# Converting the weights two units at a time, each pair joined in its own raw bytes

## The chip, the core and the metric

One core of a Trainium2 chip. The metric is the device time of one execution in microseconds. The kernel before takes 903.28 us (median of three runs, 903.13 to 905.31). All times below come from one profiled execution of it or from these runs. Five engines work beside each other and are synchronised by semaphores: TensorE (PE) multiplies matrices, VectorE (DVE) and ScalarE (ACT) work on elements, GpSimd (POOL) does the sums and maxima over partitions, and SyncE (SP) issues the transfers (DMAs). Each takes its own instructions strictly in the order in which they were written down.

## What is computed

An attention with a decay, whose result is the input of a layer that takes the maximum of three products:

```python
scores = scale * np.matmul(q, k.transpose(0, 1, 3, 2))       # 8 batches, 8 heads, 576 x 64
cum = np.cumsum(np.log(np.clip(f, 0.0001, 1.0)), axis=-1)
scores = np.where(causal, -1000000000.0, scores + cum[:, :, :, None] - cum[:, :, None, :])
attn = np.exp(scores - np.max(scores, axis=-1, keepdims=True))
attn = attn / (np.sum(attn, axis=-1, keepdims=True) + 1e-09)
x = np.matmul(attn, v)                                       # seen as [4608, 512]
h = np.maximum(np.maximum(x @ w1, x @ w2), x @ w3)           # w1, w2, w3: [512, 768]
out = (h @ w_out).astype(np.float32)                         # w_out: [768, 512]
```

The four weights arrive as float64, everything else as float32.

## The kernel before

**Weights.** They are read as pairs of int32 and cut into 24 units of 128 x 512 values: 18 of w1, w2 and w3 (four row blocks of 128 x 128 columns each; unit `step` belongs to matrix `step % 3` and column block `step // 3`) and 6 of w_out (128 rows each). `load_weights` handles one unit a call: a DMA of 0.5 MB brings the raw words into the unit's own slot `w0` to `w23` (L511); ACT rescales the top words (a Prelu, L515); DVE shifts the low words into a small tile `x` (L517) and joins top and low there to a float32 value (L519); ACT copies the value, rounded to the matmul's format, as the unit's high part (L522); DVE subtracts that from the value for the low part (L523). `x` is one of two tiles that take turns, named `o` and `hdl` in the profile. Both parts are written over the slot's raw words, which are dead by then. Each product of the last layer is three matmuls: high x high, high x low, low x high (L964 for w1 to w3, L993 for w_out).

**Attention of the first batch.** The weights are needed from the first batch's layer on, and are converted while its eight heads (numbers 0 to 7) run. A head comes in two units: unit 2, queries 0 to 255, and unit 1, the other 320, itself in two halves, first "b" (banks `s11` and `s12`), then "a" (bank `s10`). Each part is a chain over the engines: PE's first pass makes the scores (L647), DVE takes the maximum over the blocks (`mx`, L704 and L707), POOL the maximum over the partitions (`gm`, an all-reduce, L717), PE's second pass subtracts it (`s<-gm`, L647), ACT takes the exponential (`pf`, L735), PE multiplies by the values (`t` or `mp`, L772), and ACT copies the result and its sum out (`u` L784, `ph` L786). The q and k of the eight heads are read raw into the last eight weight slots and turned by PE and copied (L481 on DVE, L483 on ACT) into the tiles `ks`, `qs`, `xh` and `xl`; the last two heads' copies go to `xl`.

**The order.** A planner in Python lists steps with engine, cost in ns, keys that they read and write, and a priority; `emit` simulates the engines with these costs and writes the steps down by their simulated start. So a changed cost or key shifts steps of every engine's program. In the simulation an engine takes the ready step of the lowest priority number; weights have `WP + WR * step`, heads `n * 0.5 - LEAD`. Twenty warm-up matmuls (L453) with priority 90 fill places where PE would be idle in that simulation. SP issues all DMAs in order; an issue that must wait for a slot holds those behind it.

```python
LEAD, MLAG, WP, WR = 2.1, -0.1, 0.7, 0.65
for n in range(H):
    retire([f"raw{n}/0", f"raw{n}/1"], [f"w{NW - H + n}"])
for wstep in range(4 * FT):
    load_weights(wstep, WP + WR * wstep)
```

## Time and profile before

| | before |
|---|---|
| time, median of three runs | 903.28 us (903.13 to 905.31) |
| span of the profiled execution | 900.3 us |
| around the span (903.28 − 900.3) | 3.0 us |
| HBM read / written | 50.22 MB / 9.87 MB |
| weight units, each one DMA | 24 of 0.5 MB |
| conversion of the weights | first Prelu at 24.87 us, last subtraction at 109.2 us |

The profiled execution's own time was not recorded beside its span; the span is set against the median. "Busy" is the time in which an engine has an instruction under way; the instructions of one engine overlap by their ends, so the pitch from one start to the next is shorter than a duration. A row of a timeline shows start, duration, engine, line, operation, what is written and read, shapes, a count where equal neighbours were joined and, in brackets, idle time ahead of it with the engine that ended it.

### The profile page before, as it was taken

The numbers are of one execution on the slowest core, as the hardware profiler recorded it, in microseconds if no ns is written. First come the engines' busy times: TensorE is split into PE (matmuls) and PEld (weight loads), VectorE is DVE, ScalarE is ACT, GpSimd is POOL, SyncE is SP. The second block draws the span as 40 slices with busy tenths as digits, with TensorE's granted clock in tenths as the row PEclk, the third lists the DMA queues.
The fourth block names the chain that finished last, engine by engine and source line by source line (L and its number), as shares of the span: only waits on it lengthen the run. The fifth ranks groups of instructions, "written<-read, shape, count | busy, mean of one in ns | idle before, by whom it ended". The sixth has DMA issues, their size and how long they took to land.

```text
span 900.3 us, 18339 instructions
## 1 busy us (share of the span) xinstructions
PE 889.3 (99%) x6646; PEld 804.0 (89%) x6646; DVE 624.8 (69%) x1419; ACT 389.0 (43%) x904; POOL 425.8 (47%) x380
## 2 busy tenths in 40 slices
PE   8999999999999999999999999999999999999998
PEld 6899989888889899989989998998989898998998
DVE  6999954667759786877849787786958677672211
ACT  6898543433334443443334443344433533442111
POOL 4543232245555756556464755555565564650000
PEclk9999999999999999999999999999999999999999
DMA  7994265554464454446445445536434555401000
GB/s 197 316 270 133 56 159 131 147 135 127 99 189 96 124 136 118 126 100 169 96 124 149 117 133 138 140 93 181 95 102 123 126 149 118 105 15 37 1 36 24
DMA packets 98155, 110.99 MB, mean 123 GB/s; under 512 B 52637, under 2 KB 65693, under 8 KB 98066
## 3 DMA queue, kind: packets, MB, share of 16 engines
q1 hardware_dynamic: 98066, 109.83, 46.7%
q8 instruction: 53, 0.87, 0.4%
q14 instruction: 36, 0.29, 0.1%
HBM read 50.22 MB, written 9.87 MB: 67 GB/s over the span
## 4 chain that ended last, share of the span: by engine, by line
PE 92%; ACT 3%; DMA 1%; DVE 1%; SPq 1%; issue 1%; DVEq 0%; ACTq 0%
PE mp L964 51%; PE mp L993 17%; PE s L647 12%; PE t L803 9%; PE t L772 2%; PE t L822 1%; DMA w<-in_moe_w_dram 1%; ACT w L515 1%; ACT pf L735 1%; SPq L368 1%; DMA r_r<-rdram 0%; ACT ph L786 0%; ACT w_r L522 0%; PE s L663 0%; ACT u L784 0%
## 5 line engine op out<-in xcount | busy, mean ns | idle before, releaser
L964 PE MATMUL mp<-xh_r,w_r 128*128 128x320 f32 (+1 forms) x2160 | 463.5, 298 | 1.7 <-DVE tm L973 1.4
L964 PEld LDWEIGHTS mp<-xh_r,w_r 128*128 128x128 f32 x2160 | 356.1, 188 | 11.2 <-issue 5.6
L964 PE MATMUL mp<-xl_r,w_r 128*128 128x320 f32 (+1 forms) x1080 | 319.6, 296 | 0.4 <-DVE xl_r L940 0.4
L759 POOL PARTITION_ALL_REDUCE z<-va_s x96 | 194.9, 2030 | 158.4 <-DVE va_s L751 57.4
L717 POOL PARTITION_ALL_REDUCE gm<-mx x131 | 156.6, 1196 | 206.8 <-DVE mx L707 88.9
L964 PEld LDWEIGHTS mp<-xl_r,w_r 128*128 128x128 f32 x1080 | 203.3, 188 | 1.1 <-DVE xl_r L940 0.6
L973 DVE TENSOR_TENSOR tm<-mp,tm 128x256 f32<-128x256 f32 (+1 forms) x192 | 86.5, 451 | 84.6 <-PE mp L964 79.4
L647 PE MATMUL s<-qs_r,ks_r 128*128 128x320 f32 (+4 forms) x784 | 133.1, 284 | 0.2 <-issue 0.2
L647 PEld LDWEIGHTS s<-qs_r,ks_r 128*128 128x128 f32 (+1 forms) x784 | 116.9, 181 | 18.2 <-issue 13.4
L993 PE MATMUL mp<-w_r,hmh_r 128*128 128x512 f32 (+1 forms) x396 | 122.7, 392 | 0.0
L707 DVE TENSOR_TENSOR mx<-mx,s 128x320 f32<-128x320 f32 (+3 forms) x248 | 92.3, 372 | 19.5 <-PE s L647 6.9
L993 PEld LDWEIGHTS mp<-w_r,hmh_r 128*128 128x128 f32 x396 | 70.2, 188 | 13.2 <-issue 1.4
L976 ACT ACTIVATE hmh_r<-tm 128x256 fp32r<-128x256 f32 x96 | 39.9, 416 | 97.0 <-DVE tm L973 96.1
L993 PE MATMUL mp<-w_r,hml_r 128*128 128x512 f32 (+1 forms) x198 | 76.8, 388 | 0.0
L971 ACT ACTIVATE tm<-mp 128x256 f32<-128x256 f32 (+1 forms) x96 | 39.6, 413 | 82.3 <-PE mp L964 78.0
L536 DVE STREAM_TRANSPOSE hl<-hl 128x576 f32<-128x576 f32 x56 | 68.7, 1242 | 8.1 <-DMA hl<-in_k_dram 5.3
L735 ACT ACTIVATE pf<-s 128x512 f32<-128x512 f32 (+4 forms) x107 | 49.4, 506 | 30.5 <-PE s L647 26.4
L978 DVE TENSOR_TENSOR hml_r<-tm,hmh_r 128x256 fp32r<-128x256 f32 x96 | 48.2, 502 | 18.5 <-ACT hmh_r L976 17.9
L720 POOL CAST qs_r<-gm 1x256 fp32r<-1x256 f32 (+1 forms) x112 | 56.0, 500 | 7.2
L676 DVE TENSOR_TENSOR s<-s,mask 128x256 f32<-128x256 f32 x96 | 40.8, 425 | 25.8 <-PE s L647 25.5
L714 ACT ACTIVATE mx<-s 128x320 f32<-128x320 f32 (+1 forms) x64 | 26.7, 417 | 58.4 <-DVE s L681 45.1
L735 ACT ACTIVATE ph_f<-s 128x384 f32<-128x384 f32 x80 | 36.1, 505 | 36.1 <-PE s L647 36.1
(209 smaller groups left out, 1227.9 us busy)
## 6 DMA issues: line engine op xcount, KB each, us to landing
qs_r<-hl SPq DMA_DIRECT2D x168, 144.0 KB
ks_r<-hl SPq DMA_DIRECT2D x168, 144.0 KB
w<-in_moe_w_dram SPq DMA_DIRECT2D x18, 512.0 KB
out_dram<-o_r SPq DMA_DIRECT2D x35, 256.0 KB
hl<-in_q_dram SPq DMA_DIRECT2D x14, 576.0 KB
hl<-in_k_dram SPq DMA_DIRECT2D x14, 576.0 KB
r_r<-rdram SPq DMA_DIRECT2D x56, 144.0 KB
vn<-in_v_dram SPq DMA_DIRECT2D x30, 128.0 KB
```

The costliest lines, as they stand in the source:

```text
L536: add("DVE", 1085, lambda e=e, tt=tt, xs=xs: nc.vector.transpose(tt[:, e], xs[:, e]), [key + "0"], [key + "1"], prio)
L647: nc.tensor.matmul(bank[bk][0:l.shape[-1], col:col + w], l, rhs(qa, w), start=start and bk not in begun, stop=stop, skip_group_check=True)
L707: nc.vector.tensor_tensor(mt[:, a:a + w], mt[:, a:a + w], bank[bk][:, col:col + w], op=ALU.max)
L717: add("POOL", 450 + 2.6 * nq, lambda: nc.gpsimd.partition_all_reduce(gm, mt, P, bass.bass_isa.ReduceOp.max), [km, km + "a"], [kg], prio - CB)
L720: add("POOL", 130 + 0.9 * nq, lambda: nc.gpsimd.tensor_copy(QS(s)[96:97, 1, q0:q0 + nq], gm[96:97, :]), [kg], [kx], prio - CB)
L735: add("ACT", act_cost(w), lambda bk=bk, w=w, col=col: nc.scalar.activation(px()[:, col:col + w], bank[bk][:, 0:w], AF.Exp, scale=sc), [kb[ ...
L759: add("POOL", 520 + 5.1 * nq, lambda: nc.gpsimd.partition_all_reduce(Z[:, q0:q0 + nq], blocks_sum()[:, q0:q0 + nq], P, bass.bass_isa.Reduc ...
L803: nc.tensor.matmul(t[D * j:D * j + D, qa:qa + w], vn[:, j, c, 0:D], prs[j][0]()[:, col:col + w], start=x == 0, stop=True, skip_group_check ...
L964: nc.tensor.matmul(m, unit_w(i, fb)[:, w, kt, :], xx, start=kt == 0 and x == 0, stop=kt == KT - 1 and x == 2,)
L973: add("DVE", dve_cost(cn), lambda m=m: nc.vector.tensor_tensor(t, m, t, op=ALU.max), [km, kt_], [kt_], prio)
L978: add("DVE", dve_cost(w), lambda hh=hh, hl=hl, a=a, d=d, w=w: nc.vector.tensor_tensor(hl()[:, fb, d:d + w], t[:, a:a + w], hh()[:, fb, d:d ...
L993: nc.tensor.matmul(mp[:, 0:cn], l[:, fb, cs], unit_o(fb)[:, r, ds], start=fb == 0 and x == 0, stop=fb == FT - 1 and x == 2,)
```

## The change

The 24 slots become 12 of twice the size. A step now converts two units at once, the two neighbouring column blocks of one matrix (or two row blocks of w_out): eleven such steps, and a function `load_last` that handles the last two units of w_out singly. For a double step:

- one DMA of 1 MB (13 weight DMAs in all instead of 24) brings the raw words into slot `step + 1`;
- the Prelu, the shift, the join, the copy and the subtraction take 1024 columns each;
- the shift writes onto the low words that it reads (every second word), and the join writes the values into the first half of the same slot, so no tile `x` is used;
- the two parts are written into slot `step`, the one beside it, whose raw words were the previous step's.

So a step's split must wait for the previous step's split, and slot 11 gets raw words twice: those of step 10, and then those of the last two units, whose DMAs wait for step 10's conversion; these two use the tiles `x` as before. The order in which the steps are listed to the planner is kept, with priority `WP + 2 * WR * step`, and the costs are those of 1024 columns; for the shift in place the cost is 0.53 ns a column.

```diff
     NW = 3 * FT + FT
-    RAW = [sb(f"w{i}", [P, 1024], I32) for i in range(NW)]
+    NW2 = NW // 2
+    RAW2 = [sb(f"w{i}", [P, 2, 1024], I32) for i in range(NW2)]
+    RAW = [RAW2[i // 2][:, i % 2] for i in range(NW)]
...
+    def convert(x, low, top, kt, kl, kx, prio):
+        n = x.shape[-1]
+        add("ACT", act_cost(n) + 40, lambda: nc.scalar.activation(
+            top.bitcast(F32), top.bitcast(F32), AF.Prelu, scale=2.0 ** -112, alpha=2.0 ** 32), [kt], [kt], prio)
+        y = low if kl == kt else x
+        add("DVE", 0.53 * n + 60 if y is low else 0.85 * n, lambda: nc.vector.tensor_scalar(
+            y, low, 29, None, op0=ALU.logical_shift_right), [kt], [kl], prio)
+        add("DVE", 1.1 * n + 60, lambda: nc.vector.scalar_tensor_tensor(
+            x, top, 3, y, op0=ALU.logical_shift_left, op1=ALU.bitwise_or), [kt, kl], [kx], prio)
+
+    def split(x, h, l, kx, kh, kl, gone, prio):
+        n = x.shape[-1]
+        add("ACT", act_cost(n) + 40, lambda: nc.scalar.activation(h(), x.bitcast(F32), AF.Copy), kx, [kh] + gone, prio)
+        add("DVE", 1.1 * n + 60, lambda: nc.vector.tensor_tensor(
+            l(), x.bitcast(F32), h().bitcast(F32), op=ALU.subtract), kx + [kh], [kl], prio)
...
-        PD = 12
-        raw, x = RAW[step], XW[step % len(XW)]
+        PD = 6
+        raw, key = RAW2[step + 1].rearrange("p t x -> p (t x)"), f"w{step + 1}"
+        x = raw[:, 0:1024]
         after = [f"wh{step - PD}"] if step >= PD else []
...
-            add("SP", 560, lambda: nc.sync.dma_start(out=cols(raw), in_=src.bitcast(I32)[:, :, 2 * c0:2 * c1]),
-                after, [key], DPW + 0.01 * step, 524288 / 360)
+            add("SP", 560, lambda: nc.sync.dma_start(
+                out=raw.rearrange("p (c x) -> p c x", c=n), in_=src.bitcast(I32)),
+                after, [key], DPW + 0.02 * step, 1048576 / 360)
             pair = raw.rearrange("p (x t) -> p x t", t=2)
-            top, low = pair[:, :, 1], pair[:, :, 0]
-            add("ACT", act_cost(512) + 40, lambda: nc.scalar.activation(
-                top.bitcast(F32), top.bitcast(F32), AF.Prelu, scale=2.0 ** -112, alpha=2.0 ** 32), [key], [key], prio)
-            add("DVE", 335, lambda: nc.vector.tensor_scalar(
-                x, low, 29, None, op0=ALU.logical_shift_right), [key], [kx], prio)
-            add("DVE", 602, lambda: nc.vector.scalar_tensor_tensor(
-                x, top, 3, x, op0=ALU.logical_shift_left, op1=ALU.bitwise_or), [key, kx], [kx], prio)
-        val = cols(x.bitcast(F32))
-        add("ACT", act_cost(512) + 40, lambda: nc.scalar.activation(half(0), val, AF.Copy), [kx], [kh, key], prio)
-        add("DVE", 602, lambda: nc.vector.tensor_tensor(half(1), val, half(0).bitcast(F32), op=ALU.subtract),
-            [kx, kh], [kl], prio)
+            convert(x, pair[:, :, 0], pair[:, :, 1], key, key, key, prio)
+        split(x, lambda: both(step)[:, 0], lambda: both(step)[:, 1], [key], f"wh{step}", f"wl{step}", [f"w{step}"], prio)
+
+    def load_last(prio):
+        step = NW2 - 1
+        for e in range(2):
+            raw, x = RAW[2 * step + e], XW[e]
...
+                add("SP", 560, lambda raw=raw, src=src: nc.sync.dma_start(out=raw, in_=src.bitcast(I32)),
+                    [], [key, f"w{step}"], DPW + 0.02 * step, 524288 / 360)
+                pair = raw.rearrange("p (x t) -> p x t", t=2)
+                convert(x, pair[:, :, 0], pair[:, :, 1], key, kx, kx, prio + 0.5 * e)
+        for e in range(2):
+            split(XW[e], lambda e=e: unit_o(FT - 2 + e)[:, 0], lambda e=e: unit_o(FT - 2 + e)[:, 1],
+                  [f"x{e}"], f"wh{step}/{e}", f"wl{step}/{e}", ["wu0", "wu1"], prio + 0.5 * e)
...
-    for wstep in range(4 * FT):
-        load_weights(wstep, WP + WR * wstep)
+    for wstep in range(NW2 - 1):
+        load_weights(wstep, WP + 2 * WR * wstep)
+    load_last(WP + 2 * WR * (NW2 - 1))
```

PE's program holds the same matmuls as before. The order differs from about 25 us to about 250 us of the old trace, on every engine. Three places of it follow; a row has the line in the code, the operation, the tile that is written, `<-`, the tiles that are read (names with a running number) and the shape.

On ACT, at the first unit of the weights (in the old trace at 24.87 us), before:

```order
L483 ACTIVATE xl_70<-mp1_131 64x288
L515 ACTIVATE w0_95<-w0_95 128x512
L483 ACTIVATE xl_70<-t_129 64x288 x2
L483 ACTIVATE xl_70<-mp2_132 64x288
L515 ACTIVATE w1_96<-w1_96 128x512
L522 ACTIVATE w0_r_447<-o_120 128x512
L784 ACTIVATE u0_88<-t_129 64x160
```

and after, where L495, L501 and L812 are the old L483, L515 and L784:

```order
L495 ACTIVATE xl_70<-mp1_119 64x288
L495 ACTIVATE xl_70<-t_117 64x288 x2
L495 ACTIVATE xl_70<-mp2_120 64x288
L501 ACTIVATE w1_96<-w1_96 128x1024
L812 ACTIVATE u0_88<-t_117 64x160
L814 ACTIVATE ph1_79<-t_117 1x160
```

The copies of the last turned heads now stand ahead of the first Prelu, and there is one Prelu where there were two.

On DVE, around the maxima of head 4 "b" (`s11`, `s12`) and head 3 "a" (`s10`), in the old trace from 52.00 to 58.31 us, before:

```order
L519 SCALAR_TENSOR_TENSOR o_120<-w6_101,o_120 128x512
L704 TENSOR_REDUCE mx1_82<-s11_126 128x160
L707 TENSOR_TENSOR mx1_82<-mx1_82,s12_127 128x160
L707 TENSOR_TENSOR mx1_82<-mx1_82,s12_127 128x64
L523 TENSOR_TENSOR w5_r_711<-hdl_119,w5_r_711 128x512
L523 TENSOR_TENSOR w6_r_727<-o_120,w6_r_727 128x512
L517 TENSOR_SCALAR hdl_119<-w7_102 128x512
L517 TENSOR_SCALAR o_120<-w8_103 128x512
L519 SCALAR_TENSOR_TENSOR hdl_119<-w7_102,hdl_119 128x512
L519 SCALAR_TENSOR_TENSOR o_120<-w8_103,o_120 128x512
L704 TENSOR_REDUCE mx1_82<-s10_125 128x160
L707 TENSOR_TENSOR mx1_82<-mx1_82,s10_125 128x32
```

and after, where L504, L506 and L512 are shift, join and subtraction, L732 and L735 the maximum, and a slot number counts pairs:

```order
L504 TENSOR_SCALAR w7_102<-w7_102 128x1024
L506 SCALAR_TENSOR_TENSOR w6_101<-w6_101 128x1024
L506 SCALAR_TENSOR_TENSOR w7_102<-w7_102 128x1024
L504 TENSOR_SCALAR w8_103<-w8_103 128x1024
L890 TENSOR_SCALAR hdl_107<-mp2_120 128x8
L732 TENSOR_REDUCE mx1_82<-s11_114 128x160
L735 TENSOR_TENSOR mx1_82<-mx1_82,s12_115 128x160
L735 TENSOR_TENSOR mx1_82<-mx1_82,s12_115 128x64
L891 RECIPROCAL hdl_107<-hdl_107 128x8
L512 TENSOR_TENSOR w4_r_714<-w5_100,w4_r_714 128x1024
L732 TENSOR_REDUCE mx1_82<-s10_113 128x160
L735 TENSOR_TENSOR mx1_82<-mx1_82,s10_113 128x32
```

Ahead of the maximum on `s10` stand 9 shifts, 9 joins and 7 subtractions of one unit before, and 8, 7 and 5 of two units now; between the two maxima stand six instructions of one unit before, and now a reciprocal and one subtraction of two.

On PE, between the second pass of head 4 "b" and that of head 3 "a" (in the old trace 58.36 to 61.64 us), before:

```order
L647 MATMUL s12_127<-gm1_84,pl2_72 128x64
L964 MATMUL mp0_130<-pl1_xa_665,w0_r_447 128x256
L964 MATMUL mp0_130<-u4_92,w0_r_447 128x256
L964 MATMUL mp0_130<-pl1_xa_665,w0_r_447 128x256
L772 MATMUL mp2_132<-hmh_86,va1_78 65x128
L772 MATMUL mp2_132<-hmh_86,va1_78 65x256
L964 MATMUL mp0_130<-pl1_xa_665,w0_r_447 128x256
L964 MATMUL mp0_130<-u4_92,w0_r_447 128x256
L964 MATMUL mp0_130<-pl1_xa_665,w0_r_447 128x256
L647 MATMUL s11_126<-xh_69 128x160 x3
L647 MATMUL s10_125<-gm1_84,pl2_72 128x160 x3
L647 MATMUL s10_125<-gm1_84,pl2_72 128x32
```

and after, where L675, L800 and L886 are the old L647, L772 and L858:

```order
L800 MATMUL t_117<-pf1_80,hdh_76 65x160 x4
L886 MATMUL mp2_120<-hdl_107,rx_109 128x128 x2
L675 MATMUL s11_114<-gm1_84,pl2_72 128x160 x3
L675 MATMUL s12_115<-gm1_84,pl2_72 128x160
L675 MATMUL s12_115<-gm1_84,pl2_72 128x64
L675 MATMUL s10_113<-gm1_84,pl2_72 128x160 x3
L675 MATMUL s10_113<-gm1_84,pl2_72 128x32
L886 MATMUL mp2_120<-hdl_107,rx_109 128x128 x2
L675 MATMUL s11_114<-xh_69 128x160 x3
```

The two second passes, with other work between them before, now follow each other directly.

More of the change, by code (lines that the diff above doesn't have):

```diff
@@ L348, in blocks_sum, with both, key_w, key_o @@
         return lazy("va1", [P, S], F32, "s")
+    def both(s):
+        return lazy(f"w{s}", [P, 2, 1024])
     def unit_w(i, fb):
-        return lazy(f"w{3 * fb + i}", [P, 2, KT, P])
+        return both(3 * (fb // 2) + i).rearrange("p t (c e x) -> p t c e x", c=KT, e=2)[:, :, :, fb % 2]
     def unit_o(fb):
-        return lazy(f"w{3 * FT + fb}", [P, 2, DM])
+        return both(3 * FT // 2 + fb // 2).rearrange("p t (e x) -> p t e x", e=2)[:, :, fb % 2]
+    def key_w(i, fb):
+        return [f"{c}{3 * (fb // 2) + i}" for c in ("wh", "wl")]
+    def key_o(fb):
+        s = 3 * FT // 2 + fb // 2
+        return [f"{c}{s}" + f"/{fb % 2}" * (s == NW2 - 1) for c in ("wh", "wl")]
     TM = [sb(f"tm{i}", [P, S1]) for i in range(2)]
@@ L1062 @@
     for n in range(H):
-        retire([f"raw{n}/0", f"raw{n}/1"], [f"w{NW - H + n}"])
-    for wstep in range(4 * FT):
-        load_weights(wstep, WP + WR * wstep)
+        retire([f"raw{n}/0", f"raw{n}/1"], [f"w{(NW - H + n) // 2}"])
+    for wstep in range(NW2 - 1):
+        load_weights(wstep, WP + 2 * WR * wstep)
+    load_last(WP + 2 * WR * (NW2 - 1))
     fbs = range(FT)
```

28 lines of the change are left out of this document (13 added, 15 removed).

## The prediction

> **What bounds the kernel now.** I read the head of the page first, then the table of busy times by stretch, then what TensorE waits for.
>
> ```profile
> span 900.3 us, 18339 instructions
> PE 889.3 (99%) x6646; PEld 804.0 (89%) x6646; DVE 624.8 (69%) x1419; ACT 389.0 (43%) x904; POOL 425.8 (47%) x380
> PE 92%; ACT 3%; DMA 1%; DVE 1%; SPq 1%; issue 1%; DVEq 0%; ACTq 0%
> ```
>
> TensorE (PE) is busy for 99% of the span and makes 92% of the chain that ends last. A change that leaves PE's 6646 matmuls alone, as this one does, can only move the 11 us in which PE is idle, or add to them. The first two lines say how much room there is, not where.
>
> ```profile
> core 0: us, PE busy (x) PEld busy (x) DVE busy (x) ACT busy (x) POOL busy (x), PEclk, DMA share, GB/s
> 0.00:25.00 25.00, 21.81 (x262) 17.17 (x263) 16.26 (x37) 14.56 (x32) 12.03 (x31) 1.00 0.75 215
> 25.00:64.00 39.00, 36.99 (x296) 34.32 (x295) 36.72 (x75) 37.08 (x83) 21.14 (x22) 1.00 1.05 287
> 64.00:110.00 46.00, 46.00 (x398) 45.93 (x398) 42.22 (x95) 32.24 (x75) 14.46 (x15) 1.00 0.38 113
> 110.00:900.30 790.30, 784.54 (x5697) 706.57 (x5695) 529.62 (x1216) 305.07 (x716) 378.20 (x313) 1.00 0.44 113
> ```
>
> The averages of 69% for VectorE (DVE) and 43% for ScalarE (ACT) hide the stretch that matters. From 25 to 64 us, where the weights are converted between the first batch's heads, DVE is busy for 36.72 of 39.00 us and ACT for 37.08, and PE loses 39.00 − 36.99 = 2.0 us. From 64 to 110 it loses nothing, and the 5.8 us behind 110 lie where the conversion is over. PE's granted clock is 1.00 everywhere.
>
> ```profile
> PE t L772 <- ACT pf L735: 1.1, 2, 0.5
> PE t L772 <- ACT xl L483: 0.6, 1, 0.6
> PE s L647 <- ACT pf L735: 0.3, 1, 0.3
> ```
>
> These are PE's waits from 20 to 70 us, and they are the 2.0 us: exponentials that ACT delivers late, and once the copies of the last two turned heads. What the change can gain stands in these rows.
>
> **What the conversion costs by itself.** The pitch of neighbours (start to start) is the price of an instruction in a full queue, since the durations overlap.
>
> ```profile
> 47.18 1.25 ACT L515 ACTIVATE w<-w 128x512 f32<-128x512 f32 x2
> 70.97 0.64 ACT L522 ACTIVATE w_r<-hdl 128x512 fp32r<-128x512 f32 x1
> 71.48 0.64 ACT L522 ACTIVATE w_r<-o 128x512 fp32r<-128x512 f32 x1
> L522 ACT ACTIVATE w_r<-o x12: 612/632/645, 28.4 to 103.4; 128x512 fp32r<-128x512 f32 x12
> L540 ACT ACTIVATE hl<-hl x28: 1152/1171/1195, 31.9 to 751.9; 128x1152 fp32r<-128x1152 f32 x28
> ```
>
> ACT at 512 columns: two Prelus take 1.25 us and one 0.68, so the pitch is 0.57; the copy's is 71.48 − 70.97 = 0.51. From 512 to 1152 columns the median rises from 632 to 1171 ns, 0.84 ns a column, so 512 more cost 0.43. A Prelu of 1024 is then 1.00 (two of 512: 1.14) and a copy 0.94 (1.02). A pair saves 0.22 us, eleven pairs **2.4 us of ACT**.
>
> ```profile
> 54.29 0.68 DVE L523 TENSOR_TENSOR w_r<-hdl,w_r 128x512 fp32r<-128x512 f32 x1
> 54.89 0.94 DVE L523 TENSOR_TENSOR w_r<-o,w_r 128x512 fp32r<-128x512 f32 x1
> 55.76 0.42 DVE L517 TENSOR_SCALAR hdl<-w 128x512 int32<-128x512 int32 x1
> 56.09 0.42 DVE L517 TENSOR_SCALAR o<-w 128x512 int32<-128x512 int32 x1
> 56.43 0.68 DVE L519 SCALAR_TENSOR_TENSOR hdl<-w,hdl 128x512 int32<-128x512 int32 x1
> 57.03 0.68 DVE L519 SCALAR_TENSOR_TENSOR o<-w,o 128x512 int32<-128x512 int32 x1
> L519 DVE SCALAR_TENSOR_TENSOR o<-w,o x12: 678/689/1093, 26.0 to 101.7; 128x512 int32<-128x512 int32 x12
> L542 DVE SCALAR_TENSOR_TENSOR hl<-hl x28: 1284/1350/1762, 33.1 to 754.9; 128x1152 fp32r<-128x1152 f32 x28
> ```
>
> DVE at 512: shift 0.34 (55.76, 56.09, 56.43), join 0.60 (56.43, 57.03, 57.63), subtraction 0.60 (54.29, 54.89). From 689 to 1350 ns over 640 columns is 1.03 a column, 0.53 for 512 more: join and subtraction of 1024 cost 1.13 each (two of 512: 1.20). The shift runs at twice that pace; if it keeps it, 512 more columns cost 0.27 and it takes 0.61 (two: 0.68). A pair saves 0.21, eleven **2.3 us of DVE**. But the new shift writes onto the words it reads, 8 bytes apart, and no row shows such an instruction. At the pace of one column a time it takes as long as a join, 1.13, which is 0.52 worse. I take 0.61, since the nearest row, the same operation reading the same words 8 bytes apart, has it at the double pace; 1.13 is the other end.
>
> [...]
>
> **The front: one wait goes.**
>
> ```profile
> 24.87 0.68 ACT L515 ACTIVATE w<-w 128x512 f32<-128x512 f32 x1 [4.03 <-DMA w<-in_moe_w_dram]
> 28.39 0.61 ACT L522 ACTIVATE w_r<-o 128x512 fp32r<-128x512 f32 x1
> 58.94 0.36 PE L964 MATMUL mp<-pl_xa,w_r 128*128 128x256 f32 x1
> ```
>
> ACT waits 4.03 us for the first unit, with the `xl` copies queued behind it for which PE waits 0.6. The new order has these copies ahead of the first Prelu, so this stall goes. The first DMA is now 1 MB; at the 287 GB/s of the stretch its second half lands 0.52 / 0.287 = 1.8 us later, near 26.7. That costs nothing: the first split stands at 28.39 and PE's first matmul on a weight at 58.94, 30 us later.
>
> ```profile
> L523 DVE TENSOR_TENSOR w_r<-hdl,w_r x12: 676/684/1144, 37.7 to 109.2; 128x512 fp32r<-128x512 f32 x12
> L993 PE MATMUL mp<-w_r,hmh_r x396: 278/394/505, 118.4 to 896.4; 128*128 128x512 f32 x186, 128*128 128x256 f32 x12
> ```
>
> At the other end the last two units' DMAs must now wait on SP until slot 11 is free of step 10's raw words, and the small loads of the heads' sums queue behind them. The last unit was done at 109.2 and the first matmul on w_out starts at 118.4, so 9 us cover it; beyond these, a late unit costs PE what it is late. I cost it at nothing.
>
> **The middle: DVE is late for the heads' maxima.** The order shows the weights' work moved ahead of the maxima of the last heads. The place is the second pass of head 3 "a" (`s10<-gm`).
>
> ```profile
> 57.63 0.65 DVE L704 TENSOR_REDUCE mx<-s 128x160 f32<-128x480 f32 x1
> 58.31 0.19 DVE L707 TENSOR_TENSOR mx<-mx,s 128x32 f32<-128x32 f32 x1
> 58.36 0.75 PE L647 MATMUL s<-gm,pl 128*128 128x160 f32 x5
> 58.67 1.29 POOL L717 PARTITION_ALL_REDUCE gm<-mx  x1 [0.46 <-DVE mx L707]
> 61.64 0.62 PE L647 MATMUL s<-gm,pl 128*128 128x160 f32 x4
> 62.62 0.69 DVE L523 TENSOR_TENSOR w_r<-hdl,w_r 128x512 fp32r<-128x512 f32 x1 [0.66 <-ACT w_r L522]
> 63.84 0.88 PE L772 MATMUL t<-pf,hdh 128*65 128x32 f32 x6 [0.53 <-ACT pf L735]
> 63.69 0.19 DVE L863 RECIPROCAL hdl<-hdl 128x8 f32<-128x8 f32 x1
> 63.80 0.60 DVE L704 TENSOR_REDUCE mx<-s 128x160 f32<-128x480 f32 x1
> ```
>
> Ahead of the maximum at 57.63 the old order has 9 shifts, 9 joins and 7 subtractions: 9 × 0.34 + 16 × 0.60 = 12.7 us. The new one has 8, 7 and 5 of double size: 8 × 0.61 + 12 × 1.13 = 18.4. So DVE reaches it 5.8 us later by its own work, while PE has about as much ahead of the pass as before (some 330 matmuls into its program in both). Against this stand the slack of 61.64 − (58.67 + 1.29) = 1.7, and DVE's idle time that the work can fill: 2.28 in the stretch, less the 0.66 at 62.62 that lies behind, 1.6. The pass is late by 5.8 − 1.7 − 1.6 = 2.5 us; PE's stall of 0.53 at 63.84 is then absorbed, which leaves **+2.0 us**. If none of the idle time can be filled it is +3.6.
>
> A second count, without the slack: in the old order PE has six matmuls on w0, a head's values and a first pass between head 4 b's second pass and this one, 2.7 us (58.94 to 61.64); in the new order it has nothing. DVE has there a reciprocal, a subtraction of 1024 and the maximum: 0.11 (63.69 to 63.80) + 1.13 + 0.65 + 0.11 = 2.0, against 58.94 − 58.36 = 0.58 of PE. Were head 4 b just in time, PE would still wait 1.4; less 0.53 that is +0.9, my lower end. Behind 64 us PE's idle time is nil already, so what is lost here comes back nowhere, and with the savings of ACT and DVE nothing more is lost.
>
> **Rivals.** First, **the gain comes through**: DVE's idle time and the 2.4 and 2.3 us saved keep the maxima in time, and all of PE's stalls in the stretch go: −2.0, so 901.3. For it speak ACT's 97% and that every stall names ACT; against it that ACT was late because of what DVE and POOL gave it. Even all 2.0 us are less than 0.3%, so it needs more from behind 110 us, where the order differs up to about 250, to be told from no change.
>
> Second, on the slow side, **POOL waits behind the longer two-input instructions**.
>
> ```profile
> 35.90 0.79 POOL L717 PARTITION_ALL_REDUCE gm<-mx  x1 [2.36 <-DVE mx L707]
> 58.42 0.68 DVE L523 TENSOR_TENSOR w_r<-hdl,w_r 128x512 fp32r<-128x512 f32 x1
> ```
>
> The all-reduce of a maximum takes 0.79 us at 35.90, where DVE was done, and 1.29 at 58.67, when DVE had begun a subtraction at 58.42. The 0.5 more fits a wait for the rest of it. A subtraction of 1024 lasts 0.53 longer, and right behind the maxima the order still has one. If that is added for each of the five heads' parts in which DVE comes late (3 b, 2 a, 4 b, 3 a, 5 a) it is 5 × 0.53 = 2.6 more: 907.9. It decides where DVE, not PE, is the later one at a second pass, which is what I forecast; where PE has slack it costs nothing.
>
> [...]
>
> Third, **the shift in place loses its double pace**: 8 × 0.52 = 4.2 us more ahead of the same maximum, 905.3 + 4.2 = 909.5.
>
> **How the numbers follow.** The profiled execution spans 900.3 us, the median of the runs is 903.28; 3.0 us lie around the span, and I add the sum to 903.28: **905.3**. Some 0.3%, 2.7 us, is what a measurement can tell from no change: below 900.6 is faster, above 906.0 slower. The forecast (904.2 to 906.9) has 0.50, of which 0.12 lies above 906.0. The gain has 0.22, of which 0.06 is below 900.6. POOL's wait has 0.18 and the slow shift 0.10, both slower. So faster 0.06, same 0.38 + 0.16 = 0.54, slower 0.12 + 0.18 + 0.10 = 0.40. The range 901.0 to 909.0 takes in all but the slow shift's full price and the gain's far end, 0.16 together.
>
> **What would show it.** Prelu near 1.0 in pitch, join and subtraction 1.13, shift 0.61; ACT's 4.03 us of waiting for the first unit ends in a Prelu behind the `xl` copies, and PE's 0.6 is gone; at `s10<-gm` of head 3 PE waits for POOL's `gm`, one to three us, and DVE is busy without gaps up to there; 64 to 110 us stays full, and behind 118 us no matmul waits for w_out. If PE's idle time in 25 to 64 us falls below 2.0 us, the middle part is wrong and the first rival right; if the all-reduces behind the maxima take over 1.3 us, the second; a shift of 1.1 us, the third.

## The result, and the profile after

The changed kernel takes **910.85 us** (median of five runs, 910.2 to 914.53) against 903.13 (five runs, 900.91 to 905.31): ratio 1.0084, interval 1.0058 to 1.011. That is 7.7 us slower, above the predicted range. The profiled execution took 910.85 us itself, its span is 909.0, so 1.85 us lie around it.

The head of its page:

```profile
span 909.0 us, 18296 instructions
PE 892.6 (98%) x6646; PEld 806.0 (89%) x6646; DVE 625.6 (69%) x1386; ACT 385.9 (42%) x882; POOL 432.1 (48%) x380
PE 88%; DVE 3%; ACT 2%; DMA 1%; issue 1%; POOL 1%; SPq 0%; DVEq 0%; ACTq 0%
```

ACT is busy 3.1 us less than before and DVE 0.8 us more, and neither matters: PE's share of the chain fell from 92 to 88%. The table of busy times by stretch (us; then each engine's busy time and instructions, granted PE clock, DMA share, GB/s) shows where:

```profile
25.00:64.00 39.00, 34.58 (x269) 31.54 (x268) 36.96 (x59) 36.21 (x67) 21.39 (x19) 1.00 1.04 312
64.00:110.00 46.00, 45.31 (x391) 45.20 (x390) 36.42 (x70) 28.86 (x64) 19.15 (x16) 1.00 0.23 67
150.00:200.00 50.00, 50.00 (x418) 43.76 (x418) 29.20 (x64) 21.00 (x52) 13.05 (x16) 1.00 0.52 131
200.00:250.00 50.00, 46.90 (x321) 43.44 (x319) 37.41 (x86) 19.06 (x46) 26.81 (x22) 0.97 0.47 120
```

and the kernel before, in the last of these stretches:

```profile
200.00:250.00 50.00, 49.28 (x339) 44.55 (x338) 34.20 (x83) 19.18 (x47) 26.30 (x23) 1.00 0.47 121
```

PE idles 4.4 us from 25 to 64 us (before 2.0), 0.7 from 64 to 110 (before nothing), and 3.1 from 200 to 250 (before 0.7), where its clock is lower as well. I matched each matmul of the last layer's first product (the n-th of its kind) in the two traces: the changed kernel is **3.1 us behind at 103 us, 4.4 at 199, 8.5 at 228**, and 8.9 at the end. (The two profiles' spans differ by 8.7 us, the medians of the runs by 7.7.) So there are two losses, an early and a late one, a hundred microseconds apart.

**The early loss.** PE's waits from 20 to 120 us in the changed kernel (the line that waits, the one waited for, us in total, times, longest):

```profile
PE s L675 <- ACT pf L763: 1.6, 3, 0.8
PE mp L886 <- ACT rx L879: 1.5, 1, 1.5
PE mp L875 <- ACT ph L814: 0.8, 1, 0.8
PE s L675 <- POOL gm L745: 0.7, 1, 0.7
PE t L800 <- ACT pf L763: 0.6, 2, 0.4
```

The wait that I forecast, for the maximum of head 3 "a", is the fourth row and the smallest but one: 0.69 us. The largest single wait is in the round trip of the first four heads' sums: PE adds them up, DVE takes the reciprocal, ACT copies it to `rx`, PE spreads it. Both kernels have these two steps of PE; before (two rows) and after (five rows) on the timeline (start, duration, engine, line, operation; in brackets the idle time and what ended it):

```profile
42.23 0.56 PE L847 MATMUL mp<-hdl,ph 97*128 97x4 f32 x4
45.92 0.61 PE L858 MATMUL mp<-hdl,rx 128*128 128x128 f32 x4
```

```profile
38.66 0.61 PE L875 MATMUL mp<-hdl,ph 97*128 97x4 f32 x4 [0.79 <-ACT ph L814]
41.08 0.19 DVE L891 RECIPROCAL hdl<-hdl 128x8 f32<-128x8 f32 x1
40.91 1.05 ACT L511 ACTIVATE w_r<-w 128x1024 fp32r<-128x1024 f32 x1
41.86 0.41 ACT L879 ACTIVATE rx<-hdl 128x256 f32<-128x256 f32 x1
42.32 0.71 PE L886 MATMUL mp<-hdl,rx 128*128 128x128 f32 x4 [1.48 <-ACT rx L879]
```

The trip takes 3.7 us in both (42.23 to 45.92, 38.66 to 42.32). Before, PE had other matmuls for all of it; now it runs out of them 1.5 us early. And on ACT the copy to `rx`, whose input was there at 41.08 + 0.19 = 41.27, stands behind a weight copy until 41.86. The sums also come 3.6 us earlier than before: the planner wrote another order, not only longer steps.

**The late loss.** The timeline of PE, then of SP, DVE and ACT, at the wait for `xh`, the high part of the next layer's input, in the changed kernel:

```profile
209.99 0.42 PE L992 MATMUL mp<-xh_r,w_r 128*128 128x320 f32 x1 [2.73 <-ACT xh_r L966]
```

```profile
198.27 1.14 SPq L901 DMA_DIRECT2D rdram<-sc  x2
202.95 2.73 SPq L901 DMA_DIRECT2D r_r<-rdram  x2
208.40 0.82 DVE L961 TENSOR_TENSOR u<-u,r_r 128x576 f32<-128x576 f32 x1 [1.99 <-DMA r_r<-rdram]
209.25 0.68 ACT L966 ACTIVATE xh_r<-u 128x576 fp32r<-128x576 f32 x1 [4.52 <-DVE u L961]
```

and before:

```profile
196.53 1.18 SPq L873 DMA_DIRECT2D r_r<-rdram  x2
201.44 0.83 DVE L933 TENSOR_TENSOR u<-u,r_r 128x576 f32<-128x576 f32 x1 [1.43 <-DMA r_r<-rdram]
```

The reciprocals' load is issued 6.4 us later and DVE's product starts 7.0 later, while PE was only 4.4 behind: it waits 2.73 us. This is the second batch's work, ninety microseconds after the conversion ended. The stretches around it:

```profile
204.00:208.00 4.00, 3.26 (x23) 3.06 (x21) 2.08 (x7) 0.44 (x1) 3.70 (x3) 1.00 0.47 154
208.00:212.00 4.00, 1.63 (x6) 1.41 (x7) 1.84 (x4) 1.76 (x4) 1.35 (x3) 0.87 0.44 113
212.00:216.00 4.00, 4.00 (x22) 4.00 (x22) 2.04 (x6) 1.72 (x6) 2.44 (x3) 0.71 0.02 4
216.00:220.00 4.00, 4.00 (x34) 2.89 (x33) 3.57 (x9) 1.79 (x5) 2.15 (x1) 1.00 0.93 213
```

Behind the wait PE is busy for all of 212 to 216 us, at a clock of 0.71: 22 matmuls where the next slice has 34. The clock costs 4 × 0.13 + 4 × 0.29 = 1.7 us, and with the 2.4 us more of idle time in 200 to 250 that is the 4.1 us of the late loss.

### The profile page after: what moved, and what is told of

Read it like the earlier page. It is cut to its first block, busy times and chain, and to the rows that moved or that the text cites. A ratio compares the mean times of both kernels' runs of the same rounds, so it can differ in the third digit from the quotient of the medians.

```text
span 909.0 us, 18296 instructions
## 1 busy us (share of the span) xinstructions
PE 892.6 (98%) x6646; PEld 806.0 (89%) x6646; DVE 625.6 (69%) x1386; ACT 385.9 (42%) x882; POOL 432.1 (48%) x380
## 4 chain that ended last, share of the span: by engine, by line
PE 88%; DVE 3%; ACT 2%; DMA 1%; issue 1%; POOL 1%; SPq 0%; DVEq 0%; ACTq 0%
PE mp L992 48%; PE mp L1021 16%; PE s L675 12%; PE t L831 9%; PE t L800 1%; PE t L850 1%; DVE hl L564 1%; POOL gm L745 1%; DMA vn<-in_v_dram 1%; DVE va_s L779 0%; DMA r_r<-rdram 0%; ACT w L501 0%; DVE mx L735 0%; DVE hdl_r L1006 0%; DVE tm L1001 0%
## 5 line engine op out<-in xcount | busy, mean ns | idle before, releaser
L745 POOL PARTITION_ALL_REDUCE gm<-mx x131 | 161.1, 1232 | 207.6 <-DVE mx L732 77.2
L675 PEld LDWEIGHTS s<-qs_r,ks_r 128*128 128x128 f32 (+1 forms) x784 | 117.3, 182 | 19.5 <-issue 13.8
L675 PE MATMUL s<-qs_r,ks_r 128*128 128x320 f32 (+4 forms) x784 | 133.6, 286 | 0.3 <-POOL qs_r L748 0.3
L735 DVE TENSOR_TENSOR mx<-mx,s 128x320 f32<-128x320 f32 (+3 forms) x248 | 92.2, 372 | 21.4 <-PE s L675 7.3
```

Of the source, the lines that this page charges most:

```text
L675: nc.tensor.matmul(bank[bk][0:l.shape[-1], col:col + w], l, rhs(qa, w), start=start and bk not in begun, stop=stop, skip_group_check=True)
L735: nc.vector.tensor_tensor(mt[:, a:a + w], mt[:, a:a + w], bank[bk][:, col:col + w], op=ALU.max)
L745: add("POOL", 450 + 2.6 * nq, lambda: nc.gpsimd.partition_all_reduce(gm, mt, P, bass.bass_isa.ReduceOp.max), [km, km + "a"], [kg], prio - CB)
```

## The experiments

The kernel before took 903.3 to 903.6 us beside them. Three theories stood against each other: **width** (long instructions hold up the heads' small ones, or POOL), **slots** (values in place, each split waiting for the one before, slot 11 used twice), and **order** (the planner, given new costs and keys, writes a worse program).

### Long instructions cut in two, the order kept

In halves_new_order each of the five operations runs as two neighbouring instructions of 512 columns, in the changed kernel's order; in two_input_halves only the join and the subtraction do.

```diff
...
-        add("DVE", 1.1 * n + 60, lambda: nc.vector.scalar_tensor_tensor(
-            x, top, 3, y, op0=ALU.logical_shift_left, op1=ALU.bitwise_or), [kt, kl], [kx], prio)
...
+        def join():
+            for c in [slice(c, c + 512) for c in range(0, n, 512)]:
+                nc.vector.scalar_tensor_tensor(
+                    x[:, c], top[:, c], 3, y[:, c], op0=ALU.logical_shift_left, op1=ALU.bitwise_or)
...
+        add("DVE", 1.1 * n + 60, join, [kt, kl], [kx], prio)
...
```

> The changed kernel with its order, slots and 1 MB transfers, but each of the five operations of a weight step is issued as two instructions of 512 columns one behind the other. Theory 'order': the loss stays, and the pairs cost 0.22 us of ACT and 0.21 of DVE more each, so 910 to 914 us. Theory 'width': POOL's all-reduces get in between the halves (those above 1.5 us fall to 1.0 to 1.3), and the first part of the loss, 3 us, goes: 905 to 908 us.

> The changed kernel with only its two-input operations of DVE (join and subtraction) issued as two instructions of 512 columns; shift, Prelu and copy stay at 1024. Theory 'POOL waits behind the long two-input instructions' (my second rival): all-reduces of 1.7 to 2.0 us fall to 1.0 to 1.3, and one to three us come back: 908 to 910 us. Theory 'order': no change beyond 0.07 us a join or subtraction, 910 to 912 us.

Measured: 915.52 us, ratio 1.0129 (1.0112 to 1.0147), and 914.39, 1.0117 (1.0102 to 1.0133), slower than either theory had it. POOL's all-reduces from 22 to 100 us took 27.98 us before (25 of them), 31.29 in the changed kernel (24), and 25.65 (24) with all five operations halved. With only the join and the subtraction halved, POOL is busy for 32.39 us from 25 to 110, its other work included, against 40.54 in the changed kernel and 32.90 with all five halved. So the all-reduces are longer beside the long two-input instructions, and shortening them gave no time back. These two kernels are 4.7 and 3.5 us slower than the changed one, and what the pieces cost in themselves isn't known, so by themselves they can't rule width out; the kernels with 22 units, below, do.

### The old order with the new steps

In wide_old_order all steps but the weights' are emitted in the order of the kernel before, and a double step where its second unit stood. The planner's sort is replaced by a table of due numbers, one for each step, which the steps' dependencies overrule where they must:

```diff
-        for i in sorted(range(n), key=lambda j: (begin[j], j)):
...
+        left = [len(s[3]) for s in self.steps]
+        go = [(due[i], i) for i in range(n) if not left[i]]
+        heapq.heapify(go)
+        while go:
+            _, i = heapq.heappop(go)
             self.steps[i][2]()
+            for u in users[i]:
+                left[u] -= 1
+                if not left[u]:
+                    heapq.heappush(go, (due[u], u))
```

> The changed kernel's double-width weight steps, but every other step of every engine stands in the order of the kernel before, and a weight step of pair s stands where the second of the (2s)th and (2s+1)th single units stood. Theory 'order' (the loss comes from where the planner puts things once the weight steps have new costs and keys): PE's idle time from 25 to 64 us falls from the changed kernel's 4.4 to about 2 us or less, the 2.7 us wait for xh near 207 us is gone and the clock stays at 1.00: 901 to 904 us. Theory 'width' (the longer instructions themselves hold POOL and the heads' maxima up): the first part of the loss stays, +3 us at the first layer's last matmuls, while the late wait may go: 906 to 908 us.

It took 911.93 us, 1.0096 (1.0077 to 1.0116), no better, and outside what either theory had; but the loss is another one. The late wait is gone. Instead ACT stands behind the last two units, whose DMAs must wait for slot 11, and PE behind ACT:

```profile
110.17 0.67 ACT L516 ACTIVATE w<-w 128x512 f32<-128x512 f32 x1 [4.27 <-DMA w<-in_moe_w_out_dram]
112.54 0.68 ACT L516 ACTIVATE w<-w 128x512 f32<-128x512 f32 x1 [1.71 <-DMA w<-in_moe_w_out_dram]
113.11 0.42 ACT L778 ACTIVATE pf<-s 128x320 f32<-128x320 f32 x1
113.58 0.64 PE L690 MATMUL s<-qs_r,ks_r 128*128 128x320 f32 x1 [6.46 <-ACT pf L778]
```

Two more put 512-wide instructions on exactly the old places, with the new slots and the DMAs of 1 MB: narrow_new_slots with the value in place, narrow_x_apart with the value in the small tiles `x` (where the shift writes too), so that no split waits for the step before. The heart of the second:

```diff
-            top, low, v = pair[:, c, 1], pair[:, c, 0], x[:, c]
-            k = f"{key}/{u}"
+            top, low, v = pair[:, c, 1], pair[:, c, 0], XW[u]
+            k, kx = f"{key}/{u}", f"x{u}"
...
```

> The changed kernel's slots, 1 MB transfers, in-place shift and last two units, but every operation of a weight step is 512 columns wide and stands exactly where the single unit's operation stood in the order of the kernel before; all other steps stand in that order too. Theory 'width' (blocks of about 1.1 us in the in-order queues of ACT and DVE make the heads' chains late): no loss in the first layer, 902 to 905 us, PE's idle time from 25 to 64 us near 2.0 us. Theory 'slots' (the loss comes from the new slots: transfers of 1 MB, a split that waits for the one before, the last two units that wait for slot 11): the loss stays, 906 to 911 us, and PE waits behind ACT's wait for the last transfers.

> As the run with narrow operations in the new slots and the old order, but the values are joined in the two small tiles again, as before the change; raw words still land beside, in transfers of 1 MB. So a split needs only the joins of the step before, not its subtractions. Theory 'chain' (ACT's copy of a step has to wait for DVE's subtraction of the step before, because the joined values lie in the slot it writes, and everything behind the copy in ACT's queue waits too; 4.5 us of such waits in that run): these waits vanish and the time returns to 902 to 905 us. Theory 'transfers and slots' (1 MB, or the last units that wait for slot 11): it stays at 909 to 912 us.

Measured: 911.44 us, 1.0085 (1.0069 to 1.0101), and 908.6, 1.0049 (1.0027 to 1.007), the second between its two expected ranges. With the value in place the 103-us matmul is 3.7 us late, with `x` apart 0.1: at 512 columns on the old places ACT's copies wait 4.5 us in all for the previous step's subtraction. Both then lose about 5 us from 110 to 150, at the last two units and at loads late on SP behind their DMAs; about 1.6 us of it is the clock, 0.96 in that stretch (40 × 0.04). So slots can cost as much as the whole loss, in an order that wasn't made for them.

weights_later keeps the changed kernel and only gives the weights a higher priority number, to undo their hurry:

```diff
-    LEAD, MLAG, WP, WR = 2.1, -0.1, 0.7, 0.65
+    LEAD, MLAG, WP, WR = 2.1, -0.1, 2.2, 0.65
```

> The changed kernel with the weights' priority number raised by 1.5 heads (2.2 for 0.7), so that the planner puts the heads' maxima first again. Theory 'the planner runs the weights too early, because nothing like the two small tiles holds them back': DVE reaches the maxima earlier and the first part of the loss shrinks to 0 to 1.5 us; the late part may come or go, since the order behind 150 us shifts with it: 903 to 908 us. Theory 'width': the first part stays at 3 us.

It took 912.15 us, 1.01 (1.0078 to 1.0122), above both expectations: no help. A number for all weights moves everything at once.

### Width and order apart, with slot 11 used once

To take the reuse of slot 11 out, four kernels convert only 22 units; the last layer takes two other units of w_out in place of the last two, so the output isn't the reference's, and the matmuls are as many as before.

```diff
     def unit_o(fb):
+        fb %= 4
```

no_last_units_before is the kernel before with this. no_last_units_wide_old_order has double steps in the old order, each in its own slot, with the values in two wide tiles in slot 11; no_last_units_chain_old_order has the double steps as the change makes them, in place and each in the slot beside, in the old order. no_last_units_wide is no_last_units_wide_old_order with the planner's sort put back, and differs from it in nothing else:

```diff
-        while go:
-            _, i = heapq.heappop(go)
+        for i in sorted(range(n), key=lambda j: (begin[j], j)):
             self.steps[i][2]()
```

> The kernel before, in its order, with the last two of the 24 weight units left out (neither loaded nor converted; the second product uses two others in their place). It is the measure for the next two. Both theories: 901 to 903.5 us, since these units end 9 us ahead of their use.

> Double-width steps without the chain: raw words and both parts in a step's own slot, the values joined in two tiles of 1024 columns that lie in the slot of the last two units, which are left out (neither loaded nor converted; two others are used in their place); all other steps in the order of the kernel before. Theory 'chain': within 1.5 us of the kernel before without these units, no wait of ACT for a subtraction. Theory 'width': 3 us or more above it, with PE waiting for exponentials that stand behind Prelus and copies of 1.1 us.

> The same double-width steps without the chain and without the last two units, but in the order that the planner finds for them. Theory 'chain': within 2 us of the kernel before without these units, or below it by up to the 2 us of PE's old stalls. Theory 'width', or 'the planner's new order': 3 us or more above it, and more where the later order ripples.

> The changed kernel's double-width steps with its chain (values joined in the slot that the next step's split writes), without the last two units (neither loaded nor converted; two others are used in their place), in the order of the kernel before. It differs from the chain-free double-width run in the old order (903.1 us) by the chain alone. Theory 'chain': ACT waits for subtractions again, and 2.5 to 5 us are lost: 905.5 to 908 us. If the chain costs nothing at double width, it stays at 902.5 to 904 us, and what the old order lost was the last two units' wait alone.

| kernel | us | ratio (interval) |
|---|---|---|
| no_last_units_before | 903.24 | 0.9997 (0.998 to 1.0015) |
| no_last_units_wide_old_order | 903.11 | 0.9998 (0.998 to 1.0015) |
| no_last_units_chain_old_order | 903.2 | 0.9997 (0.9986 to 1.0008) |
| no_last_units_wide | 912.99 | 1.0106 (1.0079 to 1.0132) |

With 22 units this settles the main question. Double width, DMAs of 1 MB, the shift in place and the chain of splits cost nothing and gain nothing that could be told from 903.24 us (the intervals reach 0.2% to either side). The same instructions in the order that the planner writes for them cost 9.9 us; in that profile some 3.4 us are the clock, 0.96 from 25 to 64 and from 64 to 110 us. POOL's all-reduces are as long in the old order: those of the maxima (131 in each kernel) take 160.9 and 160.6 us in the two double-width kernels, 161.1 in the changed kernel and 157.2 in no_last_units_before. So their length costs nothing there. The planner's order for these 22 units is not the changed kernel's own: 8.0 us are lost by 103 us and 2.3 from 199 to 228, against 3.1 and 4.1. But the waits of its profile name the places of the changed kernel again:

```profile
PE mp L868 <- ACT rx L861: 2.9, 3, 1.5
PE mp L974 <- ACT xh_r L948: 1.1, 1, 1.1
PE t L782 <- ACT pf L745: 0.9, 1, 0.9
PE mp L857 <- ACT ph L796: 0.7, 1, 0.7
```

### The late part alone

out_after_rdram moves one issue in the changed kernel, an output DMA on SP, behind the store `rdram<-sc` that it stood ahead of:

```diff
+        begin[731] = begin[1037] + 1
         for i in sorted(range(n), key=lambda j: (begin[j], j)):
```

> The changed kernel with one transfer moved on SP: near 198 us the issue of a result row, which waits for ACT's copy, stands behind the two issues that send the heads' sums out, not ahead of them. If this one place in SP's queue makes the late wait, the sums leave 1.8 us earlier, the wait for xh near 207 us falls from 2.7 to about 1 us, the clock stays higher behind it, and 2 to 4 us come back: 907 to 909 us. If not, no change.

It took 911.95 us, 1.0095 (1.0075 to 1.0115). The wait for `xh` fell from 2.7 to 1.9 us and no time came back; the theory that this one issue makes the late loss fell.

Two tables then swap all that lies behind about 160 us. new_early_old_late has the changed kernel's steps and order up to there, and the old order behind it; old_early_new_late has the kernel before, and behind 160 us the order of the changed one.

> The changed kernel with its own order up to about 160 us of the trace, and from there on the order of the kernel before. If the late part of the loss (a wait of 2.7 us for xh near 207 us and the clock of 0.87 and 0.71 behind it, 4.1 us together) is a matter of the order there, on SP above all, it goes: 906 to 907.5 us, with PE's clock at 1.00 from 200 to 250 us. If it is a matter of the first layer ending late, it stays: 910 to 912 us.

> The kernel before, instruction for instruction, in its own order up to about 160 us of its trace, and from there on in the order of the changed kernel. Theory 'the new order behind 160 us is bad by itself': the wait for xh near 205 us grows to 2 to 3 us, the clock falls behind it, and 3 to 4 us are lost: 906.5 to 908 us. Theory 'it is bad only behind an early loss, when PE reaches it at another time': 902 to 904.5 us.

Measured: 907.65 us, 1.0048 (1.0034 to 1.0063), and 906.85, 1.0037 (1.0023 to 1.0051). The two shares, 0.48 and 0.37%, make 0.85%, and the whole is 0.84%. The stretch from 200 to 250 us, first with the old order behind 160, then with the new one, with four microseconds out of it and PE's wait:

```profile
200.00:250.00 50.00, 49.28 (x344) 44.89 (x343) 37.42 (x90) 20.39 (x49) 27.03 (x23) 1.00 0.48 125
```

```profile
200.00:250.00 50.00, 47.30 (x322) 43.15 (x321) 37.82 (x89) 18.56 (x46) 27.98 (x24) 0.97 0.46 117
208.00:212.00 4.00, 4.00 (x23) 4.00 (x22) 2.14 (x6) 1.76 (x5) 2.14 (x3) 0.72 0.11 25
```

```profile
PE mp L979 <- ACT xh_r L953: 2.3, 1, 2.3
```

The late order makes its wait for `xh` and the drop of the clock behind it on the untouched kernel too: 0.3 us behind at 199 us, 4.2 at 228. With the old late order, the 6.8 us by which that profile is behind at 199 us are still 6.8 at 305. (It is further behind than the changed kernel's 4.4 because its clock is 0.91 from 35 to 45 and from 45 to 55 us, which costs 20 × 0.09 = 1.8 us, around the wait of 1.47 us for `rx`, which ends at 43.24; behind the same wait the changed kernel's clock stayed at 1.00.) So the late loss is a fault of the late order itself, not a consequence of PE's being late.

### Attempts at a repair

Moving one group: group_later has the changed kernel's order with the nine steps of the first heads' sums 4 us later in the planner's time, group_later_old_late has the old order behind 160 us besides. In both the table is the whole edit.

> The changed kernel with one group of steps moved: the nine steps that turn, invert and spread the sums of the first four heads (from PE's turn at 38.66 us of its trace to the two spreads) stand 4 us later on every engine, as late as before the change. Theory 'tight round trip' (PE runs into a chain over DVE and ACT that stands behind a join of 1.1 and a copy of 1.0 us): the waits of 0.79 for ph and 1.48 for rx go, and about 2 us come back: 907.5 to 909.5 us. If another wait takes their place: 910 to 912 us.

> Both repairs at once: those nine steps 4 us later, and from 160 us on the order of the kernel before, on the changed kernel with all its weights. If the two parts of the loss are independent, 3.3 us (measured for the late order) and about 2 us come back from 910.9: 904.5 to 906.5 us. If the first doesn't help: 907 to 909 us.

915.78 us, 1.0137 (1.0119 to 1.0155), and 912.41, 1.0107 (1.0088 to 1.0126): about 5 us worse than without the move, each, and outside both expectations. The waits for `ph` and `rx` went, and three others of 1.3 to 1.7 us took their place:

```profile
39.95 0.92 PE L690 MATMUL mp<-xl 128*128 128x256 f32 x4 [1.29 <-ACT hmh L778]
43.28 1.68 PE L815 MATMUL t<-pf,vn 128*65 128x32 f32 x8 [1.66 <-ACT pf L778]
50.82 0.39 PE L1007 MATMUL mp<-pl_xa,w_r 128*128 128x256 f32 x1 [1.38 <-ACT pl_xa L948]
```

Better tables for the whole change in the old order: wide_old_order_2 puts a double step at its first unit's place, repaired_a at the second's with the last units' work moved back, repaired_b has the last two Prelus 5 us later still.

> As the first run in the old order, but a double-width step stands where the first of its two units stood, the transfers of the last two units are issued directly behind step 10's join, and their Prelus 10 us later than there, so that ACT does not wait for them with exponentials behind it. Theory 'width': 3 us of PE's time are lost by 103 us of the trace, and that is all: 905.5 to 908 us. Theory 'order': within 2 us of the kernel before, 901 to 905 us.

> The whole changed kernel (all 24 units, its slots, chain and widths) in the order of the kernel before, each double-width step at the place of the second of its units, step 10's shift to subtraction at the first; the last two units' transfers directly behind step 10's join, their Prelus far enough behind that ACT should not wait for them. Theory 'order' (instructions, slots and chain cost nothing; the planner's order, and in the old order only the wait for the last transfers, make the loss): 902.5 to 905 us, 0.9 us or less lost by 103 us of the trace, no wait of 6.5 us behind. If ACT still waits for the last transfers with exponentials behind it: 905 to 909 us.

> As repaired_a, with the last two units' Prelus and all that follows them 5 us later still. Theory 'order': 902.5 to 905 us; if the parts of w_out are then late for the second product, PE waits for them near 120 us and it is 904 to 908 us.

909.36 us, 1.006 (1.0041 to 1.0079); 909.37, 1.0065 (1.0043 to 1.0087); 907.37, 1.0049 (1.003 to 1.0068). None came to what the theory 'order' had, 905 us at most. In the best, repaired_b, the clock is 0.93 in the first 25 us (25 × 0.07 = 1.75), but that is made up by 40 us, and at 60 us the kernel is 0.2 us ahead. At 103 us it is 1.6 us behind, with waits of PE of 1.61 us at 64.31 and 0.6 behind DVE's `tm`; no_last_units_chain_old_order, with the first of these waits, is 1.0 behind there and has made it up by 205 us. So with all 24 units the conversion isn't quite free in this order. Then repaired_b loses 4.1 us from 110 to 150, about 1.6 of it by the clock, 0.96 in that stretch. The last units' DMAs, and behind them PE:

```profile
103.59 0.83 SPq L562 DMA_DIRECT2D w<-in_moe_w_out_dram  x2
109.99 0.66 SPq L610 DMA_DIRECT2D ks_r<-hl  x1
116.94 0.41 PE L690 MATMUL s<-qs_r,ks_r 128*128 128x256 f32 x2 [2.21 <-DMA ks_r<-hl]
```

In the kernel before the last weight DMA was issued at about 69 us. Now two are issued at 103.59, once slot 11 is free, and the next heads' loads queue behind them on SP. No version was faster than the kernel before, and none with all 24 units was as fast.

## Why the prediction was wrong, point by point

**PE bounds, the savings buy nothing: right.** The first rival, that the gain comes through, was ruled out even where nothing stands against it: 903.11 and 903.2 us with 22 units against 903.24. (ACT's "97%" there should be 95%: 37.08 of 39.00 us.)

**Durations: right.** Four rows of the changed kernel, the last two with their medians (ns, between the least and the most):

```profile
48.43 1.28 DVE L504 TENSOR_SCALAR w<-w 128x1024 int32<-128x1024 int32 x2
57.37 2.34 DVE L506 SCALAR_TENSOR_TENSOR w<-w 128x1024 int32<-128x1024 int32 x2
L504 DVE TENSOR_SCALAR w<-w x11: 678/901/1101, 27.8 to 83.6; 128x1024 int32<-128x1024 int32 x11
L512 DVE TENSOR_TENSOR w_r<-w,w_r x11: 1156/1219/1626, 34.8 to 87.8; 128x1024 fp32r<-128x1024 f32 x11
```

A shift that stands alone lasts 0.68 us and two 1.28, so the pitch in place is 0.60 (forecast 0.61), and a join's, with 1.21 alone, 2.34 − 1.21 = 1.13 (forecast 1.13). The third rival, the slow shift, is refuted. What the forecast missed is that most shifts stretch, to a median of 0.90. DVE's saving of 2.3 us doesn't show in its busy time, which is 0.8 us more; ACT's is 3.1 less (forecast 2.4).

**The front: right.** The first Prelu stands behind the `xl` copies, and PE no longer waits for `xl`:

```profile
26.40 1.18 ACT L501 ACTIVATE w<-w 128x1024 f32<-128x1024 f32 x1 [1.05 <-DMA w<-in_moe_w_dram]
```

**The last two units at nothing: right for this kernel, for another reason than I gave.** No matmul on w_out waits. But it is the planner's hurry that covers them, since the 22nd unit is split at 87.8 us where it was at 102.4. In the old order the reuse of slot 11 costs 4 to 9 us (4.1 in repaired_b from 103 to 150 us, 9.0 in wide_old_order, the clock of 0.96 and 0.91 from 110 to 150 us included), on ACT or on SP and before any matmul on w_out comes, so the 9 us of slack that I named were not what counts. I had named SP's queue and not priced it.

**The middle, +2.0 (0.9 to 3.6): right in size by luck, wrong in place.** The changed kernel is 3.1 us behind at 103 us. The wait at head 3 "a" is there, but 0.69 us and not one to three, and 64 to 110 us, which was to stay full, has 0.7 us of idle time. The larger part is the round trip of the sums (0.79 and 1.48) and exponentials, which I had not looked at: I counted DVE's work ahead of one maximum, and not what PE has to do beside each of its round trips.

**The second rival, POOL behind long instructions: the longer all-reduces are there, their price is not.** All-reduces reach 2.2 us, from at most 1.82, and their sum grows by 3.3; in halves_new_order the sum is 25.65 and the time 915.52. My sign for this rival, all-reduces over 1.3 us, came true, but it was no measure of the time: the double-width kernels with 22 units take 160.9 and 160.6 us for those of the maxima, against 157.2, and 903.11 and 903.2 in all. That POOL waits for the rest of a two-input instruction was my inference from two rows (0.79 and 1.29). The runs show the length beside the width (161.1 us for the maxima in the changed kernel, 156.6 before, 156.0 and 156.7 in the two kernels with 512-wide instructions in the new slots), and none shows that it cost time.

**The step that failed** is "what is lost here comes back nowhere, and with the savings of ACT and DVE nothing more is lost", together with putting aside the 5.8 us behind 110 us because "the conversion is over" there. I had written that the order differs up to about 250 us, and gave that stretch no term. It has +4.1 us, 2.4 of waiting and 1.7 of clock, nearly all at one round trip over DRAM. With it the forecast's +2.0 would have been +6, against 7.7 measured.

**Still open.** The changed kernel falls 1.3 us further behind between 103 and 199 us, of which its waits explain nothing (against the kernel before PE idles 0.27 us more from 110 to 150 and 0.23 less from 150 to 200); in part this may lie in the matching, since matmuls that are neighbours around 103 us are 3.0 to 4.4 us late, their order having changed. Which of the planner's early placements decides isn't known: the one group that I moved made it worse. And no run has the steps of the kernel before in the changed kernel's early order; that the early loss is the order's is concluded from the kernels with 22 units, whose planned order is another.

## What to carry to other kernels

Where a planner writes the order, a change of costs or keys is a change of the whole program: compare the orders to their last difference, and at every round trip (PE to another engine or to memory and back) ask what PE has to do beside it, also where the changed step is long done. To know whether an edit or its order costs, run the new steps in the old order, and the new order with the old steps: here the first lost nothing with 22 units, the second 0.37% from its late part alone. On a full engine, time saved on its neighbours bought nothing here (903.11 and 903.2 us with 22 units, against 903.24), and a buffer used twice put a wait into an in-order queue, where it held what stood behind it (in wide_old_order 4.27 us on ACT, and 6.46 on PE behind it).

## What the runs showed of the hardware

**Behind a wait of 1.61 us the clock cost 1.7 us in one profile and nothing in another.** Two kernels with the same wait of 1.61 us at the same matmuls, wide_old_order and repaired_b, each on PE's timeline and in the four microseconds from 64:

```profile
64.41 2.08 PE L815 MATMUL t<-pf,hdh 128*65 128x32 f32 x8 [1.61 <-ACT pf L778]
64.00:68.00 4.00, 3.59 (x18) 3.41 (x19) 1.82 (x6) 2.39 (x5) 0.79 (x1) 0.57 1.02 283
```

```profile
64.31 1.15 PE L815 MATMUL t<-pf,hdh 128*65 128x32 f32 x8 [1.61 <-ACT pf L778]
64.00:68.00 4.00, 3.69 (x34) 3.70 (x35) 3.06 (x10) 3.17 (x7) 1.13 (x2) 1.00 1.01 271
```

The first falls to 0.57 and loses 4 × 0.43 = 1.7 us; the second loses nothing there. Behind the 2.73 us wait of the changed kernel the clock, 0.87 and 0.71 in two stretches of 4 us, cost 1.7 as well. This may be part of the difference between runs of one kernel: the changed kernel's were 910.2 to 910.85 us at a mean clock of 0.998, 912.69 at 0.993, and 914.53 at 0.992. It is not a simple sum, though: 0.005 of 911 us would be 4.6, and the second time is only 1.8 longer. What decides whether the clock falls behind a wait, no run here shows.

**A shift in place kept its double pace**: its pitch is 0.60 us for 1024 columns where a join's is 1.13. Its durations reach 1.10.
